# An S5/H3 mix on one core: the first chunk's folds transposed on TensorE, its key spectra ahead of the second phase, loads and columns of the beginning in another order

## The chip, the cores and the metric

The kernel runs on one core of a Trainium2 chip. The metric is the device time of one execution in microseconds (us); of several runs the median counts. Before the change it is 411.53 us, the median of 3 runs from 411.17 to 412.74 us.

## The reference

The input is a sequence `x` of 2048 rows with 1024 columns. Two branches are computed from it and mixed by a gate per row.

```python
g = sigmoid((x * gate_w).sum(-1, keepdims=True))
# A: a diagonal complex state space, 1024 states, one step per row
Lam_bar = exp(dt * Lam);  B_bar = ((Lam_bar - 1) / Lam)[:, None] * Bmat
h[t] = Lam_bar * h[t-1] + B_bar @ x[t]
a = 2 * real(Cmat @ h) + x * Dskip
# B: a short convolution over k, times v, then a long one over 2048 rows
k_shift = sum over t of 4 taps: k shifted by t rows * shift_k[:, t]
kv = k_shift * v
b = x * (irfft(rfft(kv) * rfft(ssm_k)) + kv * ssm_D)
out = g * a + (1 - g) * b
```

All inputs and the output are bfloat16.

## The kernel before, in words

**Branch A** is cut into 8 residues of the row number (`M = 8`, 256 rows each) and 4 groups of states (`NG = 4`, 256 states each, real and imaginary parts apart). `load_xT(r)` brings the rows of residue r turned by a transposing transfer. `step_unit(g, r)` (tiles `bu`) multiplies them with the prepared input matrices `BT`, 32 matmuls of 256 columns, adds the state of residue r-1 by 4 matmuls with `L`, and ScalarE copies the result to `h`. After residue 7 the state `z` goes through `scan(g)`; for all groups but the last it needs a second copy `zs` with its halves exchanged, which two transfers make that ScalarE's queue starts. `carry` (tiles `psT`) brings the scanned state into the other residues; some of these are spilled to memory from ScalarE's queue (`h_scr`) and loaded again later. `Cy` (tiles `psy`) is the output matrix; it fills the last third of the run.

**Branch B** works on 8 chunks of 128 channels. For each chunk `load_k`, `load_v` and `load_kn` bring k, v and the long kernel; `tap_unit` (tiles `taps`) does the short convolution on TensorE, `times_v` multiplies by v on VectorE. The long convolution is done by transforms of length 1024 on blocks. `fold` adds and subtracts the halves of each block on VectorE (two tiles of 128x1024), and each of the two results is turned by a transposing transfer (SBUF to SBUF, 256 KB) into `eok` (kernel) or `eov` (sequence). `spectrum_unit("K" or "V", c, cc, h)` multiplies these with the tables `CF` and `SF`, 4 matmuls of 512 columns, and ScalarE copies the result to `Kr`, `Ks` (or `Kt`) or `Vh`. `products` is the long VectorE chain (`Kp`, `G`, `tmp`, `T`), and `inverse` (tiles `psz`, then `cv`) goes back to rows and spills them to `cv_scr`, again from ScalarE's queue.

**Beginning.** `state_columns` makes the columns of branch A (tiles `cw`, `cols`), `vectors` and `more_vectors` turn small rows into columns on TensorE (tile `psp`): `pcol`, the taps `tcol` and `dcol`, the gate's column `gz`, and `sDc`. `forward_tables` makes `CF` and `SF`. `matrices(g)` makes the tiles `L` of a group on VectorE, `B_unit(q)` multiplies the loaded rows `Bst` with `L` (tiles `psB`, 8 matmuls of 128 columns) and ScalarE copies the result to `BT`.

**The gate.** `gate(r)` multiplies residue r with `gz`; ScalarE copies the row (`grow`) to SBUF, and four small transfers of GpSimd's queue put it into `glog`.

**What sets the order.** Every instruction of an engine is bound to follow the one recorded before it (`put`, line 97), so each engine works off its list in the order written. After the beginning two phases are interwoven: `weave(A[0:NS], first)` mixes the first residues of branch A with the spectra of chunk 0, and the eight periods that follow mix the rest of branch A with `period(c)`. Where a piece stands is a fraction in the table `AT` (line 929): a fraction of the period's matmul weight for branch B (`p0` to `p10` are the steps of `products`, `K00` to `V11` spectra, `fk` the kernel's fold, `lk`, `lv`, `ln` the loads), a residue's number with decimals for the rest. PSUM is one pool of four tiles of two banks, which all of these share. The transfers that SyncE's and ScalarE's queues start are counted on eight semaphores in turn, so that a transfer can be started when the one that had its semaphore before has landed; an engine whose queue holds such a start waits there with all that stands behind it. The pool `s2` has 33 tiles of 2 KB per partition; the gate's row is one of them, and the pool of `cv` has two.

Of the kernel before, what the change touches and what calls it, by code (L numbers as in the profile page):

```python
# [20 lines left out]
def kernel(  # L21
# [169 lines left out]
    small(skr, B_shift_k.rearrange("(j p) k -> j p k", p=128))  # L191
# [49 lines left out]
    def more_vectors():  # L241
        for k in range(KS):
            for h in range(2):
                o = (2 * h + k // 2) * ND
                p0 = 64 * (k % 2)
                mm(psp[p0:p0 + 64, 0, o:o + ND], skr[:, 64 * h:64 * h + 64, k], ident[0:ND, 0:ND], True, True)
        for k in range(KS):
            mm(psp[:, 0, 96 + k:97 + k], skr[:, :, k], ident[0:ND, 0:1], True, True)
        mm(psp[:, 0, 64:64 + 2 * ND], gsr, ident[0:2 * ND, 0:2 * ND], True, True)
        copy(tcol, psp[:, 0, 0:KS * ND].rearrange("p (i j) -> p i j", j=ND))  # L250
        copy(dcol, psp[:, 0, 96:96 + KS])
        copy(gz[:, :, 0], psp[:, 0, 64:64 + ND])
# [61 lines left out]
    def state_columns():  # L314
# [342 lines left out]
    def gate(r):  # L657
# [4 lines left out]
        row = s2([128, K], "grow", F32)  # L662
# [257 lines left out]
    def rows(ts_):  # L920
# [47 lines left out]
        "first": (0.399, 0.45, 0.47, 0.49, 0.51, 0.491, 0.55, 0.57),  # L968
        "gate": (1.261, 3.605, 2.943, 3.887, 4.018, 5.053, 7.446),
        "tabs": ((3.2, 5.821, 6.755, 7.95), (3.928, 5.78, 5.164, 5.561), (1.135, 4.206, 5.313, 6.2), (2.709, 3.396, 5.357, 3.91)),  # L970
        "scan": ((3.375,), (1.2, 1.461, 1.701, 4.5, 3.628, 5.574, 6.459, 6.5, 6.55, 7.5), (1.2, 1.493, 2.127, 4.5, 4.269, 6.764, 6.988, 6.5, 6.55, 7.596), (3.324, 2.57, 2.902, 5.617, 1.123, 5.385, 6.891, 6.921, 3.889, 7.5)),
        "B": ((3.393, 2.536, 7.95, 6.523, 6.218), (3.197, 4.6, 5.6, 7.631, 7.722), (4.107, 4.517, 4.004, 5.925, 7.95)),
        "C": (0.0, 0.394, 0.0, 3.014, 5.724, 0.126, 6.899, 7.218), "tailC": (0.228, 0.188),
# [241 lines left out]
```

## Time and profile before

| what | before |
|---|---|
| median of 3 runs | 411.53 us (411.17 to 412.74) |
| the profiled execution: its own time | 413.82 us |
| its span, first to last instruction | 412.0 us |
| mean granted TensorE clock | 0.984 |
| TensorE busy | 382.3 us (93%), 2598 matmuls |
| VectorE busy | 327.3 us (79%) |
| ScalarE busy | 247.7 us (60%) |
| moved by the transfers | 66.56 MB, 162 GB/s on average |

Rows of a timeline give the start, the duration, the engine (SPq, ACTq: an instruction of that engine's queue that starts a transfer), the operation with its tiles, how many of them are merged (x16), and in brackets how long the engine stood idle before it and what released it. A merged row lasts from its first start to its last end. Rows of windows give, for a stretch, each engine's busy time with its instructions, the granted TensorE clock (PEclk, 1.00 is full), the busy share of the 16 transfer engines and their GB/s.

### The profile page before, as it was taken

The numbers are of one execution on the slowest core, as the hardware profiler recorded it, in microseconds if no ns is written. First come the engines' busy times: TensorE is split into PE (matmuls) and PEld (weight loads), VectorE is DVE, ScalarE is ACT, GpSimd is POOL, SyncE is SP. The second block draws the span as 40 slices with busy tenths as digits, with TensorE's granted clock in tenths as the row PEclk, the third lists the DMA queues.
The fourth block names the chain that finished last, engine by engine and source line by source line (L and its number), as shares of the span: only waits on it lengthen the run. The fifth ranks groups of instructions, "written<-read, shape, count | busy, mean of one in ns | idle before, by whom it ended". The sixth has DMA issues, their size and how long they took to land.

```text
span 412.0 us, 6722 instructions
## 1 busy us (share of the span) xinstructions
PE 382.3 (93%) x2598; PEld 237.8 (58%) x2598; DVE 327.3 (79%) x421; ACT 247.7 (60%) x317; POOL 37.2 (9%) x77
## 2 busy tenths in 40 slices
PE   2979998999998699999998899999999999999994
PEld 1546877576766476787766665354544444444442
DVE  6846869989979699829884886999699899757754
ACT  5637577858793476765653976266833638165671
POOL 2201001224601220100012000100000000000000
PEclk9989999999999699999999999999999999999998
DMA  8999999998199737922999969993664200778862
GB/s 158 203 195 242 200 223 176 196 187 193 29 184 290 117 27 173 210 53 76 201 212 190 147 144 197 247 197 99 144 184 113 86 18 0 212 220 237 221 184 76
DMA packets 140496, 66.56 MB, mean 162 GB/s; under 512 B 121896, under 2 KB 128048, under 8 KB 140464
## 3 DMA queue, kind: packets, MB, share of 16 engines
q1 hardware_dynamic: 131920, 51.66, 60.6%
q0 software_dynamic: 3888, 6.33, 8.9%
q10 hardware_dynamic: 4656, 8.15, 6.9%
q8 instruction: 20, 0.33, 0.3%
q14 instruction: 12, 0.10, 0.1%
HBM read 19.68 MB, written 11.01 MB: 74 GB/s over the span
## 4 chain that ended last, share of the span: by engine, by line
PE 68%; DVE 11%; DMA 10%; ACT 6%; issue 2%; SPq 1%; ACTq 1%; POOL 1%; DVEq 0%; POOLq 0%
PE psy L99 24%; PE bu L99 22%; PE psV L99 5%; PE psz L99 5%; PE psK L99 5%; DMA xT<-in_A_x_dram 4%; PE psT L99 3%; DVE G L99 3%; DMA eov<-vfold 3%; PE taps L99 2%; DVE tmp L99 2%; DMA CT<-CT 2%; DVE T L99 1%; SPq L99 1%; DMA eok<-kfold 1%
## 5 line engine op out<-in xcount | busy, mean ns | idle before, releaser
L99 PE MATMUL bu<-xT,BT 128*128 128x256 bf16 x1024 | 120.2, 277 | 7.1 <-DMA xT<-in_A_x_dram 3.1
L99 PEld LDWEIGHTS <-BT 128*128 128x128 bf16 x1024 | 101.0, 99 | 26.5 <-issue 7.0
L99 PE MATMUL psy<-CT,h 128*128 128x512 bf16 x448 | 98.8, 379 | 0.7 <-DMA CT<-Cim 0.7
L99 PEld LDWEIGHTS <-h 128*128 128x128 bf16 x448 | 43.8, 98 | 53.8 <-DMA CT<-Cim 1.2
L99 ACT ACTIVATE h<-bu 128x1024 bf16<-128x1024 f32 x28 | 28.6, 1022 | 47.9 <-PE bu L99 45.4
L99 ACT ACTIVATE Vh<-psV 128x1024 bf16<-128x1024 f32 x32 | 31.5, 1033 | 5.0 <-PE psV L99 2.5
L99 DVE TENSOR_TENSOR G<-G,tmp 128x3072 bf16<-128x3072 bf16 (+2 forms) x24 | 29.4, 1225 | 0.8
L99 DVE TENSOR_TENSOR T<-T,tmp 128x3072 bf16<-128x3072 bf16 (+2 forms) x24 | 29.4, 1225 | 0.8
L99 ACT ACTIVATE h<-psT 128x1024 bf16<-128x1024 f32 x28 | 27.6, 1027 | 3.6 <-PE psK L99 1.2
L99 DVE TENSOR_TENSOR tmp<-Kp,Vh 128x3072 bf16<-128x3072 bf16 (+2 forms) x24 | 29.3, 1221 | 0.4
L99 POOL DMA_DIRECT2D kk<-kk x21 | 11.1, 532 | 189.7 <-DMA kk<-in_B_k_dram 149.5
L99 ACT ACTIVATE cv<-psz 128x1024 bf16<-128x1024 f32 x16 | 16.5, 1029 | 15.1 <-PE psz L99 7.7
L99 PE MATMUL psT<-h,ident 128*128 128x256 bf16 x112 | 25.4, 272 | 0.0
L99 PEld LDWEIGHTS <-L 128*128 128x128 bf16 x224 | 21.9, 98 | 4.5 <-issue 1.0
L99 PE MATMUL psz<-T,CI 128*128 128x512 bf16 x64 | 24.3, 379 | 0.0
L99 PE MATMUL psz<-T,SI 128*128 128x512 bf16 x64 | 24.3, 379 | 0.0
L99 PEld LDWEIGHTS <-CF 128*128 128x128 bf16 x128 | 12.4, 99 | 18.5 <-issue 6.5
L99 ACT ACTIVATE pairx<-pairx,omg 128x1024 bf16<-128x1024 bf16 (+1 forms) x12 | 11.6, 965 | 18.5 <-DMA pairx<-cv_scr 18.5
L99 DVE TENSOR_TENSOR G<-Kr,Vh 128x4096 bf16<-128x4096 bf16 x8 | 18.3, 2287 | 4.8 <-ACT Vh L99 4.8
L99 PE MATMUL taps<-kk,w 128*64 128x512 bf16 (+1 forms) x128 | 19.8, 402 | 2.0 <-ACT w L99 1.9
L99 PE MATMUL psK<-eok,CF 128*128 128x512 bf16 x64 | 16.9, 394 | 4.8 <-ACT grow L99 4.8
L99 PEld LDWEIGHTS <-SF 128*128 128x128 bf16 x128 | 11.9, 98 | 15.4 <-issue 4.1
(154 smaller groups left out, 574.8 us busy)
## 6 DMA issues: line engine op xcount, KB each, us to landing
kn<-in_B_ssm_k_dram SPq DMA_DIRECT2D x8, 512.0 KB, 4.1
cv_scr<-cv ACTq DMA_DIRECT2D x16, 256.0 KB, 3.2
kk<-kk POOLq DMA_DIRECT2D x14, 255.9 KB, 5.4
h_scr<-h ACTq DMA_DIRECT2D x10, 256.0 KB, 4.5
h<-h_scr SPq DMA_DIRECT2D x10, 256.0 KB, 3.2
CT<-Cim SPq DMA_DIRECT2D x16, 128.0 KB, 3.5
out_dram<-ga SPq DMA_DIRECT2D x16, 128.0 KB, 1.9
Bst<-in_A_B_re_dram SPq DMA_DIRECT2D x14, 128.0 KB, 3.3
```

The lines of the kernel that those rows point to most:

```text
L99: i = f(*a, **kw)
```

## The change

It has five parts.

1. The two folds of chunk 0 (`fold_first`) are no longer turned by transfers. VectorE makes both sums as before; each is multiplied, in 8 pieces of 128 columns, with the unit matrix on TensorE (tiles `psf`, 16 matmuls of 128 columns per fold and 32 in all), and ScalarE copies the four results to `eok` and `eov`.
2. The four key spectra of chunk 0 stand in the beginning, between the fold of the kernel and that of the sequence, and ahead of the second phase, which now interweaves only the four spectra of the sequence.
3. The loads of the beginning are reordered: the kernel `kn` right behind the first `xT`, then the third B rows, v, the fourth B rows, and three `xT` in a row; `B_shift_k` is loaded from SyncE's queue and no longer from ScalarE's. `more_vectors`, `state_columns` and `forward_tables` are cut at other places: `dcol`, `gz` and `sDc` behind VectorE's phase columns, `tcol` at the end of the beginning (its PSUM tile is kept until then), the tables `CF` and `SF` ahead of the tap units' copies. Of `matrices(0)` only the first tile is made ahead of the B units, which are split: two, the fold of the kernel, one, the spectra, the fold of the sequence, one.
4. The gate's row is taken from the two tiles of `cv` and no longer from `s2`.
5. Nearly all places in `AT` are new.

```diff
-    small(skr, B_shift_k.rearrange("(j p) k -> j p k", p=128))
+    move(skr, B_shift_k.rearrange("(j p) k -> j p k", p=128))
...
-        copy(tcol, psp[:, 0, 0:KS * ND].rearrange("p (i j) -> p i j", j=ND))
+        yield
         copy(dcol, psp[:, 0, 96:96 + KS])
         copy(gz[:, :, 0], psp[:, 0, 64:64 + ND])
         copy(sDc, psp[:, 0, 64 + ND:64 + 2 * ND])
+        yield
+        copy(tcol, psp[:, 0, 0:KS * ND].rearrange("p (i j) -> p i j", j=ND))
...
+    def fold_first(hi, lo, name):
+
+        eo = cbuf([128, 2, 4, 2, 128], "eo" + name)
+        fs = []
+        for op in (ALU.add, ALU.subtract):
+            fs.append(s2([128, 4, 256], name + "f"))
+            tt(fs[-1], hi, lo, op)
+        yield
+        for e, f in enumerate(fs):
+            ps = ps2([128, 8, 128], "psf")
+            for k in range(8):
+                mm(ps[:, k], flat(f)[:, 128 * k:128 * k + 128], ident, k % 4 == 0, k % 4 == 3)
+            act(eo[:, e].rearrange("p a m d -> p (a m) d"), ps, func=ACT.Copy)
+        {"k": eoks, "v": evs}[name][0] = eo
...
-        row = s2([128, K], "grow", F32)
+        row = cv_pool.tile([128, K], F32, name="grow", tag="cv")
...
-        "fk": {0: 0.679, 1: 0.504, 7: 0.812, 3: 0.304, 2: 0.146, 5: 0.703, 6: 0.639, 4: 0.494},
+        "fk": {0: 0.648, 1: 0.282, 7: 0.956, 3: 0.304, 2: 0.146, 5: 0.782, 6: 0.351, 4: 0.419},
...
     load_B(0, small)
+    load_B(1, small)
     load_k(0)
     load_xT(0)
-    load_B(1, small)
+    load_kn(0)
     load_B(2)
+    load_v(0)
     load_B(3)
-    load_kn(0)
-    load_v(0)
     load_xT(1)
+    load_xT(2)
...
-    matrices(0)
-    for q in range(4):
-        B_unit(q)
-    fold_k(0)
-    step(ft)
-    load_xT(2)
+    matrices(0, (0,))
+    fk = fold_k0()
+    step(fk)
+    run(ft)
+    B_unit(0)
+    B_unit(1)
+    run(fk)
+    B_unit(2)
+    for cc in range(2):
+        for h in range(2):
+            spectrum_unit("K", 0, cc, h)
+    run(mv)
     times_v(0)
-    fold_v(0)
+    fv = fold_v0()
+    step(fv)
+    matrices(0, (2, 4))
+    run(fv)
+    B_unit(3)
     load_xT(3)
-    run(ft)
```

ScalarE in the beginning, from the copies of the tap units (`ks`) to the first states `h`; `BT` are the input matrices, `eok` and `eov` the turned folds, `hf`, `CF` and `SF` the tables. Before:

```order
L99 ACTIVATE ks<-taps 128x1024 x2
L99 ACTIVATE grow<-p 128x2x128
L99 ACTIVATE BT<-psB 128x1024 x4
L99 ACTIVATE hf<-rq 128x512
L99 ACTIVATE CF<-hf,pih 128x2x256
L99 ACTIVATE SF<-rq 128x2x256
L99 ACTIVATE h<-bu 128x1024 x2
L99 ACTIVATE Kr<-psK 128x2x4x128 x2
L99 ACTIVATE Ks<-psK 128x2x4x128 x2
L99 ACTIVATE Vh<-psV 128x2x4x128 x4
```

and with the change:

```order
L99 ACTIVATE ks<-taps 128x1024 x2
L99 ACTIVATE grow<-p 128x2x128
L99 ACTIVATE BT<-psB 128x1024 x2
L99 ACTIVATE eok<-psf 128x1024 x2
L99 ACTIVATE BT<-psB 128x1024
L99 ACTIVATE Kr<-psK 128x2x4x128 x2
L99 ACTIVATE Ks<-psK 128x2x4x128 x2
L99 ACTIVATE eov<-psf 128x1024 x2
L99 ACTIVATE BT<-psB 128x1024
L99 ACTIVATE Vh<-psV 128x2x4x128 x3
L99 ACTIVATE h<-bu 128x1024 x2
```

The tables went ahead of `ks`, four copies of folds came in, and the fourth `BT`, without which no first state can be formed, now stands behind the four copies of key spectra and behind all four folds.

SyncE's queue in the beginning, from the fourth B rows to the second load of `kn`, as one piece of the difference (`xT` are the turned rows of a residue, `vT` is v turned):

```order
-L99 DMA kn<-in_B_ssm_k_dram 128x2048
-L99 DMA_TRANSPOSE vT<-in_B_v_dram 128x2048
-L99 DMA_TRANSPOSE xT<-in_A_x_dram 128x8x256
-L99 DMA_TRANSPOSE eok<-kf 128x8x128 x2
-L99 DMA_TRANSPOSE xT<-in_A_x_dram 128x8x256
-L99 DMA_TRANSPOSE eov<-vfold 128x8x128 x2
-L99 DMA_TRANSPOSE xT<-in_A_x_dram 128x8x256
+L99 DMA_TRANSPOSE xT<-in_A_x_dram 128x8x256 x3
```

The four turned folds are gone from the queue, and `kn` and `vT` stand further ahead.

SyncE's queue later, in the second group's last residues, the transfers of chunks 3 and 4 that end with the fold `eov` of chunk 3. Before:

```order
L99 DMA Bst<-in_A_B_re_dram 64x1024
L99 DMA Bst<-in_A_B_im_dram 64x1024
L99 DMA_TRANSPOSE eok<-kfold 128x8x128 x2
L99 DMA kn<-in_B_ssm_k_dram 128x2048
L99 DMA Bst<-in_A_B_re_dram 64x1024
L99 DMA Bst<-in_A_B_im_dram 64x1024
L99 DMA_TRANSPOSE kk<-in_B_k_dram 128x2048
L99 DMA_TRANSPOSE vT<-in_B_v_dram 128x2048
L99 DMA_TRANSPOSE eov<-vfold 128x8x128 x2
```

and with the change:

```order
L99 DMA_TRANSPOSE eok<-kfold 128x8x128 x2
L99 DMA Bst<-in_A_B_re_dram 64x1024
L99 DMA Bst<-in_A_B_im_dram 64x1024
L99 DMA_TRANSPOSE kk<-in_B_k_dram 128x2048
L99 DMA Bst<-in_A_B_re_dram 64x1024
L99 DMA Bst<-in_A_B_im_dram 64x1024
L99 DMA kn<-in_B_ssm_k_dram 128x2048
L99 DMA_TRANSPOSE vT<-in_B_v_dram 128x2048
L99 DMA_TRANSPOSE eov<-vfold 128x8x128 x2
```

The pair `eok` went ahead of both pairs of B rows, and `kk` ahead of `kn`; `vT` and `eov` are still the last two.

More of the change, by code (lines that the diff above doesn't have):

```diff
@@ L348, in state_columns @@
         tt(tl, tl, tr, ALU.subtract)
+        tt(II, ident[:, 0:64], ident[:, 64:128], ALU.add)
+        ts(jrow, jrow_i, 0.5, None, ALU.mult)
         yield
@@ L418, in fold_k, with fold @@
         hi, lo = kb[:, :, 1], kb[:, :, 0, ::-1]
-        eoks[c] = fold(hi, lo, "k", c == 0)
-    def fold(hi, lo, name, first=False):
+        eoks[c] = fold(hi, lo, "k")
+    def fold(hi, lo, name):
         eo = cbuf([128, 2, 4, 2, 128], "eo" + name)
         for e, op in enumerate((ALU.add, ALU.subtract)):
-            f = s2([128, 4, 256], "kf") if first else fold_pool.tile([128, 4, 256], BF16, name=name + "fold", tag="f")
+            f = fold_pool.tile([128, 4, 256], BF16, name=name + "fold", tag="f")
             tt(f, hi, lo, op)
@@ L459, in fold_v, with fold_k0, fold_v0 @@
         evs[c] = fold(kb[:, :, 1], kb[:, :, 0, ::-1], "v")
+    def fold_first(hi, lo, name):
[11 more added lines that the diff above has]
+        {"k": eoks, "v": evs}[name][0] = eo
+    def fold_k0():
+        kn = lds.pop(("kn", 0))
+        tt(kn[:, 0:1], kn[:, 0:1], sDc[:, 0:1], ALU.add)
+        kb = kn.rearrange("p (a h t) -> p a h t", a=4, h=2)
+        return fold_first(kb[:, :, 1], kb[:, :, 0, ::-1], "k")
+    def fold_v0():
+        kb = kss[0].rearrange("p (a h t) -> p a h t", a=4, h=2)
+        return fold_first(kb[:, :, 1], kb[:, :, 0, ::-1], "v")
     def spectrum_unit(which, c, cc, h):
@@ L929 @@
     AT = {
[38 rows of a table removed]
[L968 to L973, printed above, removed]
-        "tailS": (0.0, 0.446, 0.005, 1.22, 0.0, 1.104, 0.163, 0.262, 1.952, 2.0),
[29 rows of a table removed]
[38 rows of a table added]
+        "first": (0.038, 0.0, 0.584, 0.168), "gate": (0.184, 3.444, 1.97, 3.456, 5.383, 5.053, 7.214),
+        "tabs": ((3.2, 4.258, 6.522, 7.95), (3.928, 5.78, 5.091, 5.672), (0.0, 3.825, 5.313, 6.2), (2.634, 4.327, 5.39, 3.91)),
+        "scan": ((1.535,), (1.2, 1.461, 1.701, 4.397, 3.628, 5.574, 6.459, 6.5, 6.55, 7.5), (1.027, 1.493, 2.127, 4.5, 4.269, 6.764, 6.988, 6.994, 6.536, 7.596), (3.324, 2.861, 3.571, 5.617, 1.123, 5.048, 6.88, 6.621, 3.828, 7.5)),
+        "B": ((3.393, 3.131, 7.684, 5.345, 6.218), (3.197, 4.6, 5.6, 7.707, 7.95), (4.107, 4.517, 4.166, 5.925, 7.95)),
+        "C": (0.173, 0.394, 0.392, 3.375, 0.163, 0.483, 5.365, 6.473), "tailC": (0.0, 0.187),
+        "tailS": (0.047, 0.579, 0.048, 1.471, 0.0, 0.93, 0.144, 0.556, 1.816, 2.0),
[30 rows of a table added]
     }
@@ L1071 @@
     load_B(0, small)
+    load_B(1, small)
     load_k(0)
     load_xT(0)
-    load_B(1, small)
+    load_kn(0)
     load_B(2)
+    load_v(0)
     load_B(3)
-    load_kn(0)
-    load_v(0)
     load_xT(1)
-    sc, ft, it = state_columns(), forward_tables(), inverse_tables()
+    load_xT(2)
+    sc, ft, it, mv = state_columns(), forward_tables(), inverse_tables(), more_vectors()
     step(ft)
     vectors()
+    step(mv)
     step(sc)
-    more_vectors()
+    step(mv)
     tap_weights(0)
     step(sc)
-    step(sc)
+    step(ft)
     tap_unit(0, 0)
@@ L1116 @@
     first = [(AT["first"][i], w, f) for i, (w, f) in enumerate((
-        (WK, later(spectrum_unit, "K", 0, 0, 0)),
-        (WK, later(spectrum_unit, "K", 0, 0, 1)),
-        (WK, later(spectrum_unit, "K", 0, 1, 0)),
-        (WK, later(spectrum_unit, "K", 0, 1, 1)),
         (WK, later(spectrum_unit, "V", 0, 0, 0)),
```

3 lines of the change are left out of this document (removed), and 133 rows, old and new, of the table AT.

## The prediction

> **What bounds the kernel now.** First the page's busy times:
>
> ```profile
> span 412.0 us, 6722 instructions
> PE 382.3 (93%) x2598; PEld 237.8 (58%) x2598; DVE 327.3 (79%) x421; ACT 247.7 (60%) x317; POOL 37.2 (9%) x77
> ```
>
> TensorE is busy 382.3 of 412.0 us, so at most 29.7 us of idle time can be won, and every added matmul costs unless it fills a hole. Second, TensorE's waits, largest first (total, how often, longest):
>
> ```profile
> PE p L99 <- DVE rows L99: 5.3, 1, 5.3
> PE psK L99 <- ACT grow L99: 4.8, 1, 4.8
> PE bu L99 <- DMA xT<-in_A_x_dram: 3.1, 1, 3.1
> ```
>
> They are few, and each is one event. The first lies ahead of everything the change moves; the second and third are what it can win. Third, the timeline of the beginning (SPq: SyncE's queue):
>
> ```profile
> 8.36 1.26 ACT L99 ACTIVATE w<-ident,dcol 128x128 bf16<-128x128 bf16 x4
> 8.80 5.66 PE L99 MATMUL taps<-kk,w 128*128 128x512 bf16 x16 [1.85 <-ACT w L99]
> 14.73 1.96 PE L99 MATMUL psB<-L,Bst 128*128 128x128 bf16 x32
> 15.70 3.78 ACT L99 ACTIVATE BT<-psB 128x1024 bf16<-128x1024 f32 x4
> 16.78 3.80 PE L99 MATMUL bu<-xT,BT 128*128 128x256 bf16 x32
> 19.29 3.10 SPq L99 DMA_TRANSPOSE eok<-kf  x2
> 19.38 1.23 DVE L99 TENSOR_TENSOR ks<-ks,vT 128x2048 bf16<-128x2048 bf16 x1 [0.94 <-DMA vT<-in_B_v_dram]
> 20.64 1.29 DVE L99 TENSOR_TENSOR vfold<-ks 128x1024 bf16<-128x1024 bf16 x2
> 23.68 5.08 PE L99 MATMUL bu<-xT,BT 128*128 128x256 bf16 x32 [3.11 <-DMA xT<-in_A_x_dram]
> 24.72 2.75 SPq L99 DMA_TRANSPOSE eov<-vfold  x2
> 29.03 1.89 PE L99 MATMUL psK<-eok,CF 128*128 128x512 bf16 x8
> 33.77 3.82 ACT L99 ACTIVATE Vh<-psV 128x1024 bf16<-128x1024 f32 x4
> 35.94 3.66 PE L99 MATMUL bu<-xT,BT 128*128 128x256 bf16 x32
> ```
>
> Residue 1's `bu` waits 3.11 us for its `xT`, then its 32 matmuls last 5.08 us against 3.66 in residue 2. The windows say why (PE, PEld, DVE, ACT, POOL, then PEclk, DMA share, GB/s):
>
> ```profile
> 23.70:27.00 3.30, 3.30 (x18) 2.40 (x19) 1.63 (x2) 0.00 (x0) 0.00 (x0) 0.56 1.08 238
> 27.00:29.00 2.00, 2.00 (x21) 1.79 (x19) 0.00 (x0) 0.00 (x0) 0.00 (x0) 1.00 0.90 167
> ```
>
> After that pause the granted clock was 0.56, and within 3.3 us it was full again. Fourth, the largest movable wait, at 132 us (ACTq: ScalarE's queue):
>
> ```profile
> 113.17 4.18 SPq L99 DMA_TRANSPOSE eok<-kfold  x2
> 117.44 0.53 SPq L99 DMA_DIRECT2D kn<-in_B_ssm_k_dram  x1
> 119.33 2.76 SPq L99 DMA_TRANSPOSE kk<-in_B_k_dram  x1
> 120.92 1.29 DVE L99 TENSOR_TENSOR vfold<-ks 128x1024 bf16<-128x1024 bf16 x2
> 122.19 3.24 SPq L99 DMA_TRANSPOSE vT<-in_B_v_dram  x1
> 125.60 7.27 SPq L99 DMA_TRANSPOSE eov<-vfold  x2
> 131.19 5.37 ACTq L99 DMA_DIRECT2D zs<-z  x2
> 136.60 0.40 ACT L99 ACTIVATE grow<-p 128x256 f32<-128x256 f32 x1 [5.45 <-DMA eov<-vfold]
> 137.05 1.86 PE L99 MATMUL psK<-eok,CF 128*128 128x512 bf16 x4 [4.75 <-ACT grow L99]
> 138.71 5.59 PE L99 MATMUL bu<-xT,BT 128*128 128x256 bf16 x32
> ```
>
> SyncE starts five transposing transfers one behind the other. The chain of waits gives the last one 10.47 us, so it lands at 136.07:
>
> ```profile
> 125.60 10.47 DMA eov<-vfold
> ```
>
> ScalarE wants to start `zs`, whose semaphore is the one of `eov`; it stands 5.45 us, with `grow` behind it, and TensorE waits 4.75 us for the PSUM tile of `grow`. Then it is cold: four `psK` take 1.86 us (half of the eight in 1.89 would be 0.95, so 0.9 more), the `bu` 5.59 instead of 3.66 (1.9 more). The stall costs 4.75 + 0.9 + 1.9 = **7.5 us**.
>
> **The change part by part.** *Beginning.* Removed are four transposing transfers (1 MB; 3.10 + 2.75 us of SyncE's queue) and, with `xT` of residue 1 now behind no fold, the 3.11 us wait and its cold matmuls. But the first state is formed later: the last `BT` now stands behind four fold copies and four key spectra. From 15.70 ScalarE has 12 copies in a row (three `BT`, four folds, four key spectra, the last `BT`); by 3.78 / 4 = 0.95 us each they last 11.4 us, to 27.1. TensorE's work beside it (32 `psB` 1.96, 32 fold matmuls of the same shape 1.96, key spectra 2 x 1.89, three of the four pairs of V spectra or so) is some 8.6 us and fits: the 1.96 us that are added cost nothing while ScalarE sets the pace, and all of 1.96 if it does not. The three V spectra that stand ahead of the first states are through about 27.8. Then come two residues of `bu` (2 x 3.66) and the fourth V spectrum (half of 1.89), 8.3 in all; merged rows end with a latency that the next group overlaps, so the four small matmuls of residue 1's state are not added. Residue 2 starts at about 36.1 where it started at 35.94. **+0.2 us**. Below: if ScalarE's copies wait less than counted, -0.8; above: the beginning keeps its length and only the added 1.96 and the wait's remains come on top, +2.5. I take the middle sum, since each of its terms has a row. Covers: `xT` 1 is needed at about 31 instead of 23.7; `vT` was there at 19.4, and `ks` and the fold (1.23 and half of 1.29) must be done before ScalarE reaches `eov` at 24, so it may be 2.7 us late before anything waits; `kn`, now behind the first `xT`, is used no earlier than before. `w` waits for `dcol`, which now sits behind VectorE's phase columns; `w` starts at 8.36 today, and a delay there would move the whole front one to one.
>
> *The glut.* SyncE's order is now `eok` first, then B rows, `kk`, `kn`, `vT`, `eov`. Where the pair `eok` was started at 113.17, its place is some 11 us earlier, into a stretch with free transfer engines:
>
> ```profile
> 100.00:120.00 20.00, 20.00 (x174) 13.89 (x174) 17.00 (x19) 16.92 (x22) 9.32 (x18) 1.00 0.51 82
> 120.00:140.00 20.00, 15.25 (x120) 10.55 (x119) 16.18 (x17) 9.36 (x11) 3.72 (x7) 0.90 1.15 234
> ```
>
> The DMA share is 0.51 at 82 GB/s before 120 and 1.15 at 234 GB/s behind it. The pair is 0.5 MB: at 234 GB/s 2.2 us less stand in front of `eov`. SyncE's 4.18 us for it are gone from 113 on, and `kk` no longer waits for `kn`, but `eov` cannot start before `vfold` ends at 120.92 + 1.29 = 122.2, 3.4 us earlier than 125.60. So `eov` lands 2.2 to 5.2 us earlier (3 of start, 2.2 of bytes), and of ScalarE's 5.45 us 0.2 to 3.2 stay, middle 1.7. TensorE's wait was 0.7 shorter than ScalarE's, so 1.0 stays, too short to cool it: a wait of 1.68 us, below, was followed by `bu` at full pace. I take 7.5 - 1.1 = **-6.4 us**. Bounds: 0 if `eov` lands no earlier, -7.5 if all goes; -4.9 with 3.2 of hold left.
>
> *The gate's row* now shares two tiles with `cv`. A later `cv` must wait until the four small transfers have read the row, which stand in POOL's queue behind two `H`:
>
> ```profile
> 81.64 2.15 POOL L99 DMA_DIRECT2D H<-a  x2 [2.08 <-DVE H L99]
> 85.89 1.02 ACT L99 ACTIVATE cv<-psz 128x1024 bf16<-128x1024 f32 x1
> ```
>
> 2.15 for `H`, as much again for the row's four, and a landing of about 3.3 us end at `H` + 7.6; `cv` was copied at `H` + 4.25. ScalarE may be held 1 to 3 us, which two blocks of `bu` on TensorE (2 x 3.66) hide: 0. If the cover is gone it is up to 3.4, of the kind in the next bound.
>
> *New places.* Nearly every piece moves. The stall at 222 us has the same build after the change (`cv`'s spill still queues on the semaphore of an `eov`):
>
> ```profile
> 221.78 1.02 ACT L99 ACTIVATE cv<-psz 128x1024 bf16<-128x1024 f32 x1 [6.93 <-DMA eov<-vfold]
> 222.85 3.65 PE L99 MATMUL bu<-xT,BT 128*128 128x256 bf16 x32 [1.68 <-ACT cv L99]
> 228.10 3.65 PE L99 MATMUL bu<-xT,BT 128*128 128x256 bf16 x32 [1.59 <-ACT Kr L99]
> ```
>
> No row shows what moved places do. Below: both waits go, -1.7 - 1.6 = -3.3. Above: one more stall as long as today's largest, +4.75. I take the middle, **+0.8**, since neither end is nearer.
>
> Sum: +0.2 - 6.4 + 0.8 = **-5.4**. The profiled execution's own time is 413.82, 2.3 above the median of the runs; the sum goes onto its span, 412.0 to 406.6 (its own time to 408.4), and the same difference onto the median: 411.5 - 5.4 = **406.1 us**.
>
> **The rivals.** *The glut stays* (1): the bytes, not their order, set when `eov` lands. For it: 234 GB/s behind 120 us, whatever the queue does. Against: the stretch before has half its share free. Then +0.2 + 0.8 = 412.5.
>
> *Given back later* (2): TensorE comes 5.4 us earlier to 217 us, the transfers do not, and the hold behind `eov` grows. For it, the window there:
>
> ```profile
> 216.00:220.00 4.00, 4.00 (x37) 3.50 (x36) 3.90 (x8) 0.00 (x0) 0.52 (x1) 1.00 1.35 214
> 224.00:228.00 4.00, 2.51 (x23) 2.09 (x22) 0.82 (x2) 3.67 (x10) 0.00 (x0) 1.00 1.30 122
> ```
>
> The DMA share is 1.30 to 1.35. Against: the loads there are started by a queue that moves with the work. If all transfers stay, all 5.4 are lost, 411.5; if half move along, 408.8; I put it at 410.4.
>
> *Slower: a half clock in the front* (3). Between 15.7 and 36 us TensorE works in groups of 0.5 to 1 us between ScalarE's copies, and nothing long lets it warm. If the clock falls to half there and stays, 8.6 us of work become 17.2 in a stretch of 12, +5.2, and two residues of `bu` another 7.3: +12.5 - 5.4 = 418.6; warm again after 3.3 us as in the windows above, it is about +5. It decides if the clock is still half at 23 us. Against: 224 to 228 was 2.51 of 4.00 busy, with a clock of 1.00.
>
> The Trainium skill, "TensorE: Matmul & The Clock Gate", section "A second HAM failure mode: psum-queue depth-cycling", names this: short pauses between PSUM groups can make the clock oscillate. The trace so far speaks against it, by the row just named.
>
> **How the numbers follow.** About 2 us (0.5%) is what a measurement here tells from no change: 409.5 to 413.6. The forecast gets 0.56, all faster. (1) gets 0.12, nearly all within; (2) 0.14, of it 0.10 within and 0.04 faster; (3) 0.10, slower; 0.08 is left for what none of them names, half faster, half not. Faster 0.63, within 0.22, slower 0.15. The forecast's own range: 402.0 (both later waits go too) to 409.5 (3.2 of the hold stays, and a new stall of 2). Reaching to (1) gives **402.0 to 412.6**; (3) and part of the rest stay outside.
>
> **What would show it.** Front: ScalarE without a hole from 15.7 to about 27, `bu` of residue 2 near 36, a clock of 1.00 between; half clock at 23 us or later speaks for (3). Glut: no wait of `psK` for `grow`, ScalarE not held at `zs` for over 3.2 us, `eov` landing within 4 to 7 us of its start; if it still takes 10, (1). The waits of `bu` for `cv` and `Kr` at 217 to 223 us stay at 1 to 2 us; at 5, (2). No hold of `cv` behind `glog` over 3 us. The forecast is wrong if TensorE's idle time, 29.7 us now, is not below 27, or if a wait over 3 us stands where none stood.

## The result and the profile after

| | before | changed |
|---|---|---|
| median of 4 runs | 411.50 us (411.17 to 412.74) | 407.32 us (405.71 to 408.37) |
| the profiled execution: its own time, span | 413.82, 412.0 us | 408.37, 406.6 us |
| mean granted TensorE clock | 0.984 | 0.998 |
| TensorE busy, idle | 382.3, 29.7 us | 379.7, 26.9 us |

The changed kernel is faster by 1.1%: ratio 0.989, 95% interval 0.9851 to 0.9929. The medians differ by 4.2 us and the two profiled spans by 5.4 us. Two more timings on other chips, told below, gave 0.9946 (0.9876 to 1.0015, which includes no change) and, with the gate's row in `s2` again, 0.9909 (0.9866 to 0.9952). The gain is thus some 2 to 4.5 us, in each of the three less than the 5.4 us that were forecast. In the experiments below executions of one and the same kernel lie up to 16 us apart (the kernel before: 406.3 to 422.0), so the medians there are over all executions, while the ratios, by which faster or slower is told, leave out those over 1.5% above the fastest of their kernel.

The page of the changed kernel, to be set beside the two lines of the kernel before:

```profile
span 406.6 us, 6769 instructions
PE 379.7 (93%) x2630; PEld 238.2 (59%) x2630; DVE 326.7 (80%) x421; ACT 251.2 (62%) x321; POOL 37.2 (9%) x77
```

32 matmuls were added (rows `psf` of 1.36 and 1.06 us), and TensorE is busy 2.6 us less: the matmuls that ran at a lower clock before are shorter now. Its waits (in all, times, longest):

```profile
PE bu L99 <- ACT Kr L99: 2.9, 1, 2.9
PE psy L99 <- DMA CT<-Cim: 2.8, 2, 1.8
...
PE taps L99 <- DMA kk<-kk: 1.6, 1, 1.6
PE psK L99 <- ACT BT L99: 1.6, 1, 1.6
PE psV L99 <- ACT eov L99: 1.2, 1, 1.2
PE psK L99 <- ACT eok L99: 0.8, 1, 0.8
PE psK L99 <- ACT grow L99: 0.6, 1, 0.6
```

The 4.8 us for `grow` are 0.6, the 3.1 us for `xT` are gone, `CT` has 2.8 us where it had 0.7, and 1.6 us for `kk` are new. The beginning, from the timeline:

```profile
15.32 1.94 ACT L99 ACTIVATE BT<-psB 128x1024 bf16<-128x1024 f32 x2
17.12 1.98 ACT L99 ACTIVATE eok<-psf 128x1024 bf16<-128x1024 f32 x2
18.23 1.89 PE L99 MATMUL psK<-eok,CF 128*128 128x512 bf16 x8 [0.78 <-ACT eok L99]
...
23.45 2.06 ACT L99 ACTIVATE eov<-psf 128x1024 bf16<-128x1024 f32 x2
...
25.26 1.17 ACT L99 ACTIVATE BT<-psB 128x1024 bf16<-128x1024 f32 x1
26.16 3.02 ACT L99 ACTIVATE Vh<-psV 128x1024 bf16<-128x1024 f32 x3
...
27.23 7.15 PE L99 MATMUL bu<-xT,BT 128*128 128x256 bf16 x64
...
35.52 3.66 PE L99 MATMUL bu<-xT,BT 128*128 128x256 bf16 x32
```

and the same stretch by windows (PE, PEld, DVE, ACT, POOL, then clock, DMA share, GB/s):

```profile
15.30:27.20 11.90, 9.67 (x84) 5.89 (x83) 9.96 (x16) 11.90 (x15) 2.29 (x4) 1.00 1.13 199
```

ScalarE is busy in 11.90 of 11.90 us: it sets the pace here, TensorE has 9.67 us of work beside it, and the clock is 1.00. At 100 to 134 us:

```profile
98.56 5.08 SPq L99 DMA_TRANSPOSE eok<-kfold  x2
111.30 1.90 SPq L99 DMA_TRANSPOSE kk<-in_B_k_dram  x1
...
114.75 0.59 SPq L99 DMA_DIRECT2D kn<-in_B_ssm_k_dram  x1
117.53 1.04 POOL L99 DMA_DIRECT2D kk<-kk  x2 [1.82 <-DMA kk<-in_B_k_dram]
119.30 2.76 SPq L99 DMA_TRANSPOSE vT<-in_B_v_dram  x1
122.22 4.94 SPq L99 DMA_TRANSPOSE eov<-vfold  x2
122.55 0.52 POOL L99 DMA_DIRECT2D kk<-kk  x1 [3.98 <-DMA kk<-kk]
...
131.62 1.13 ACTq L99 DMA_DIRECT2D zs<-z  x2
133.30 1.02 PE L99 MATMUL psK<-eok,CF 128*128 128x512 bf16 x4 [0.57 <-ACT grow L99]
134.20 3.88 PE L99 MATMUL bu<-xT,BT 128*128 128x256 bf16 x32
```

`eok` starts 14.6 us earlier than before, `kk` 8.0, `eov` 3.4. ScalarE starts both `zs` in 1.13 us instead of 5.37, `psK` waits 0.57 us and is not cold (1.02 against 1.86), nor is `bu` behind it (3.88 against 5.59). The three differences are 4.18 + 0.84 + 1.71 = 6.7 us. The rows of GpSimd's queue, `kk<-kk`, are the three transfers with which `load_k` shifts k inside SBUF for the short convolution; they play a part below. The stall at 217 us stays:

```profile
215.35 1.02 ACT L99 ACTIVATE cv<-psz 128x1024 bf16<-128x1024 f32 x1 [6.48 <-DMA eov<-vfold]
221.56 3.65 PE L99 MATMUL bu<-xT,BT 128*128 128x256 bf16 x32 [2.88 <-ACT Kr L99]
```

### The profile page after: what moved, and what is told of

It is laid out like the page before. It is cut to its first block, busy times and chain, and to the rows that moved or that the text cites. A ratio compares the mean times of both kernels' runs of the same rounds, so it can differ in the third digit from the quotient of the medians.

```text
span 406.6 us, 6769 instructions
## 1 busy us (share of the span) xinstructions
PE 379.7 (93%) x2630; PEld 238.2 (59%) x2630; DVE 326.7 (80%) x421; ACT 251.2 (62%) x321; POOL 37.2 (9%) x77
## 4 chain that ended last, share of the span: by engine, by line
PE 55%; DVE 8%; ACT 4%; DMA 4%; issue 4%; SPq 1%; ACTq 1%; DVEq 0%; POOLq 0%
PE psy L99 24%; PE bu L99 15%; PE psz L99 4%; PE psV L99 4%; PE psK L99 3%; DVE G L99 3%; PE psT L99 3%; DMA CT<-CT 2%; PE taps L99 2%; ACT h L99 1%; DMA kk<-kk 1%; DVE tmp L99 1%; DVE a L99 1%; SPq L99 1%; DVE T L99 1%
## 5 line engine op out<-in xcount | busy, mean ns | idle before, releaser
L99 PE MATMUL bu<-xT,BT 128*128 128x256 bf16 x1024 | 116.9, 273 | 3.2 <-ACT Kr L99 2.9
L99 PEld LDWEIGHTS <-BT 128*128 128x128 bf16 x1024 | 99.6, 98 | 20.8 <-issue 5.3
L99 POOL DMA_DIRECT2D glog<-grow x32 | 18.1, 651 | 36.8 <-ACT grow L99 35.4
L99 ACT ACTIVATE gd<-drow,glog 128x512 bf16<-128x512 bf16 (+1 forms) x25 | 20.7, 827 | 0.0
```

What stands on the lines that cost most here:

```text
L99: i = f(*a, **kw)
```

## The experiments

Theory at the start: the stall at 132 us was what the change won, through the order of SyncE's queue there (`eok` early, `kk` ahead of `kn`); the beginning itself is worth little. First rival: the shifted beginning dissolved the stall. Below, "before" is the median of the kernel before, timed beside the experiment on the same chip.

**The beginning alone.** The changed kernel with the old table `AT` (its `first` apart) and the old place of the gate's row.

```diff
-        row = cv_pool.tile([128, K], F32, name="grow", tag="cv")
+        row = s2([128, K], "grow", F32)
...
-        "p0": {0: 0.023, 5: 0.146, 6: 0.15, 7: 0.097, 4: 0.0, 3: 0.051, 2: 0.068, 1: 0.224},
+        "p0": {0: 0.127, 5: 0.195, 6: 0.154, 7: 0.017, 4: 0.0, 3: 0.0, 2: 0.135, 1: 0.224},
...
```

> The kernel with the new beginning alone: turned folds on TensorE, key spectra ahead, loads and columns reordered; the table of places and the gate's row as before. Theory (the beginning itself is worth little, the stall at 132 us is what was won): residue 2's bu starts at 35.5 us as in the changed kernel (35.94 before), the wait of psK for grow near 135 us stays at 4 to 5 us, and the time is 411.1 us, 0 to 1 below before. Rival (shifting the beginning is what dissolved the later stall): the wait is under 1.5 us and the time is 404 to 407 us.

Measured: 411.45 us, before 413.93; ratio 1.0022 (0.9972 to 1.0072). The wait of `psK` for `grow` is 4.24 us, residue 2 starts at 35.96, residue 4 at 44.27 (45.13 before). The rival falls: with the new beginning the stall stands where it stood. What the beginning is worth by itself cannot be told from nothing by the interval.

**SyncE's order alone, in the kernel before.** One number, then two. TensorE's and ScalarE's lists stay the same word for word.

```diff
-        "fk": {0: 0.679, 1: 0.504, 7: 0.812, 3: 0.304, 2: 0.146, 5: 0.703, 6: 0.639, 4: 0.494},
+        "fk": {0: 0.679, 1: 0.282, 7: 0.812, 3: 0.304, 2: 0.146, 5: 0.703, 6: 0.639, 4: 0.494},
```

> The kernel before with one number changed: the fold of chunk 3's kernel at 0.282 of its period instead of 0.504, so that its pair eok is started some 10 us earlier; TensorE and ScalarE have the same lists. Theory (2.2 us of bytes and SyncE's 4.2 us leave the front of eov, but kn still stands ahead of kk): eov lands 2 to 5 us earlier than 136.07, psK's wait for grow falls from 4.75 to 0 to 2.5 us, time 405.5 to 409 us. Rival 1 (the bytes behind 120 us set the landing whatever the order): wait 4 us or more, 411 to 412 us.

Besides it, in the second:

```diff
-        "ln": {0: 0.996, 6: 0.979, 7: 0.252, 3: 0.63, 5: 0.943, 2: 0.522, 4: 0.559, 1: 0.64},
+        "ln": {0: 0.996, 6: 0.979, 7: 0.252, 3: 0.63, 5: 0.943, 2: 0.522, 4: 0.559, 1: 0.835},
```

> As the run before, and the load of kn at 0.835 instead of 0.64, behind that of kk: SyncE's list at this place is then the one of the changed kernel, word for word, in the kernel before. Theory: the stall is gone, wait under 1 us, bu behind it at 3.7 instead of 5.59 us, all of 7.5 us but what later waits take back: 404 to 406.5 us. Rival 2 (given back at 214 to 228 us, where the transfers do not move along): waits there grow from 3.3 to over 6 us and the time is 409.5 to 411.5 us.

Measured: the first 409.28 us, before 413.93 (ratio 0.9981, 0.9936 to 1.0026), with a wait of 0.99 us for `grow`. The short wait wins little: TensorE comes to this place at 135.11 us, 2.8 us later than in the kernel before, and `psK` starts at 136.10, only 1.0 us earlier. The second took 413.20 us (ratio 1.0067, 1.0014 to 1.0119) and is slightly slower. Unlike what was expected of it, it does not have SyncE's order of the changed kernel: `kk` stands behind both pairs of B rows, where the changed kernel has it between them, and `kn` starts 1.7 us ahead of `vT`, where the changed kernel has 4.6. Its timeline, with the last B rows:

```profile
114.17 0.59 SPq L99 DMA_DIRECT2D Bst<-in_A_B_im_dram  x1
114.94 3.68 SPq L99 DMA_TRANSPOSE kk<-in_B_k_dram  x1
118.67 0.58 SPq L99 DMA_DIRECT2D kn<-in_B_ssm_k_dram  x1
120.37 2.75 SPq L99 DMA_TRANSPOSE vT<-in_B_v_dram  x1
121.33 1.04 POOL L99 DMA_DIRECT2D kk<-kk  x2 [6.50 <-PE psV L99]
123.29 10.09 SPq L99 DMA_TRANSPOSE eov<-vfold  x2
...
140.04 0.40 ACT L99 ACTIVATE grow<-p 128x256 f32<-128x256 f32 x1 [7.30 <-DMA eov<-vfold]
140.49 1.86 PE L99 MATMUL psK<-eok,CF 128*128 128x512 bf16 x4 [6.60 <-ACT grow L99]
```

`eov` starts 2.3 us earlier than in the kernel before, and the wait is longer, 6.60 us. `vT` takes 12.2 us to land, where it took 4.8 in the changed kernel and 7.1 before. What runs beside it are the shifts `kk<-kk` and the load of `kn`. So these two numbers alone are not enough. The full order of the changed kernel is put into the kernel before further below, with an earlier second tap unit.

**The same two numbers undone in the changed kernel.**

```diff
-        "fk": {0: 0.648, 1: 0.282, 7: 0.956, 3: 0.304, 2: 0.146, 5: 0.782, 6: 0.351, 4: 0.419},
+        "fk": {0: 0.648, 1: 0.504, 7: 0.956, 3: 0.304, 2: 0.146, 5: 0.782, 6: 0.351, 4: 0.419},
...
-        "ln": {0: 0.896, 6: 0.979, 7: 0.0, 3: 0.63, 5: 0.909, 2: 0.522, 4: 0.607, 1: 0.835},
+        "ln": {0: 0.896, 6: 0.979, 7: 0.0, 3: 0.63, 5: 0.909, 2: 0.522, 4: 0.607, 1: 0.64},
```

> The changed kernel with those two numbers as before (fold of chunk 3's kernel at 0.504, load of kn at 0.64). Theory: psK's wait for grow near 133 us comes back with 3 to 5 us and a cold clock behind it, time 411 to 414 us. Rival (other new places keep the stall away by themselves): 406.5 to 408.5 us.

Measured: 419.75 us, before 413.93, ratio 1.022 (1.015 to 1.0289): slower than the kernel before.

```profile
121.33 6.18 SPq L99 DMA_TRANSPOSE vT<-in_B_v_dram  x1
122.34 1.04 POOL L99 DMA_DIRECT2D kk<-kk  x2 [8.07 <-PE psz L99]
127.69 12.34 SPq L99 DMA_TRANSPOSE eov<-vfold  x2
...
143.15 1.86 PE L99 MATMUL psK<-eok,CF 128*128 128x512 bf16 x4 [11.88 <-ACT grow L99]
```

So the changed kernel needs these places, and the price without them is above the 3 to 5 us of wait that were expected. `vT` took 19.5 us to land, again beside `kk<-kk`, with `kn` and a pair of B rows started within 2 us ahead of it. The windows compare what is moved. From 120 to 142 us this kernel's transfer engines are busy at a share of 1.16 and move 176 GB/s; the changed kernel from 117 to 133 us moves 239 GB/s at 1.06. But the kernel before, with its stall, moves 244 GB/s at 1.16 from 119 to 136 us, so there an excess of bytes is not excluded. The three, in this order:

```profile
120.00:142.00 22.00, 11.27 (x100) 8.20 (x98) 12.57 (x13) 5.83 (x6) 1.56 (x3) 0.85 1.16 176
```

```profile
117.00:133.00 16.00, 15.73 (x133) 11.42 (x131) 15.24 (x15) 10.44 (x12) 1.56 (x3) 1.00 1.06 239
```

```profile
119.00:136.00 17.00, 13.30 (x116) 9.78 (x114) 14.90 (x15) 7.85 (x8) 1.56 (x3) 1.00 1.16 244
```

**A second theory: collision** (theory C in the expectations). The shifts `kk<-kk` and the transposing `vT` and `eov` would slow each other when they run together. In the kernel before they run side by side:

```profile
125.58 1.04 POOL L99 DMA_DIRECT2D kk<-kk  x2 [12.35 <-DMA kk<-in_B_k_dram]
```

that is in the same moment as `eov` (125.60). In the changed kernel the first two start at 117.53, 1.8 us ahead of `vT`; the third starts at 122.55, beside `eov` there too. The rival is that the bytes alone count: the three shifts are 768 KB, by the 244 GB/s above some 3 us (an estimate). Three experiments go with it: the kernel with the long stall and the kernel before, each without the three shifts of chunk 4, and the kernel before with both numbers and an earlier second tap unit, which frees the buffer of `kk`.

```diff
-        if c == 0:
+        if c in (0, 4):
             return
         hop(kk[0:64, 1, PAD:], kk[64:128, 0, PAD:])
```

> The changed kernel with chunk 3's fold and the load of kn late, which took 419.75 us with a wait of 11.88 us of psK for grow; here it also leaves out the three transfers kk<-kk that shift k of chunk 4 (768 KB; chunk 4's short convolution then works on wrong rows, so part of the computation is missing). Theory C: the wait falls under 2.5 us and the time to 407 to 410.5 us, though kk, vT, kn and both pairs of folds are started as late as there. Rival 1 (bytes alone: 0.77 MB less at some 200 GB/s are 3.8 us): wait 7 to 9 us, 414.5 to 417 us.

> The kernel before without the three transfers kk<-kk of chunk 4 (chunk 4's short convolution then works on wrong rows, so part of the computation is missing), all else as it is. Theory C: eov lands within 7 us of its start instead of 10.5, psK's wait for grow falls from 4.75 to under 1.5 us, the spread becomes narrow and the median is 404 to 408 us. Rival 1 (bytes: 3.8 us at most): wait 1 to 4 us, 409 to 411 us, spread as before.

Measured: the kernel with the long stall 414.10 us (its six executions 411.4 to 416.3; with the shifts, on another chip, 417.7 to 420.2), ratio to before 1.0129 (1.0037 to 1.0222); the kernel before 410.47 us against 415.01, ratio 0.9971 (0.9907 to 1.0035). Their timelines, the first without the long stall:

```profile
120.64 4.12 SPq L99 DMA_TRANSPOSE vT<-in_B_v_dram  x1
124.93 5.51 SPq L99 DMA_TRANSPOSE eov<-vfold  x2
...
136.37 1.83 PE L99 MATMUL psK<-eok,CF 128*128 128x512 bf16 x4 [4.75 <-ACT grow L99]
```

and the kernel before without shifts:

```profile
128.02 4.36 SPq L99 DMA_TRANSPOSE eov<-vfold  x2
...
136.07 1.02 PE L99 MATMUL psK<-eok,CF 128*128 128x512 bf16 x4 [1.18 <-ACT grow L99]
```

In the first TensorE comes to this place at the same time with and without shifts (131.62 and 131.27 us), so the two waits can be compared: they are 4.75 and 11.88 us, and the shifts cost 7.1 us there, more than the 3 us of their bytes. But 4.75 us stay with no shift in the way, `vT` still takes 12.6 us, and the transfer engines move 187 GB/s, hardly more than the 176 with shifts:

```profile
120.00:142.00 22.00, 17.25 (x136) 12.33 (x135) 19.24 (x19) 10.33 (x12) 2.11 (x4) 0.92 0.96 187
```

The wait lies between theory C (under 2.5) and the rival (7 to 9); the time misses theory C by 3.6 us and the rival by 0.4. In the kernel before, the waits of 4.75 and 1.18 us can't be subtracted: without shifts TensorE comes 2.6 us later (134.89 against 132.30), and `psK` starts at 136.07, 1.0 us earlier than with them. `eov` landed at most 7.6 us after its start, against 10.5. The wait fits theory C and the rival, and the time (409 to 411) and the spread, as wide as before (406.2 to 418.0), are the rival's. So collision is not shown for the kernel before: bytes would do as much.

The kernel before with both numbers (`fk` and `ln`), and besides:

```diff
-        "t1": {0: 0.034, 1: 0.661, 7: 0.928, 6: 0.67, 3: 0.648, 5: 0.62, 4: 0.65, 2: 0.645},
+        "t1": {0: 0.034, 1: 0.61, 7: 0.928, 6: 0.67, 3: 0.648, 5: 0.62, 4: 0.65, 2: 0.645},
```

> The kernel before with fold and kn placed as in the run with both numbers changed (fold 0.282, kn 0.835), and besides the second tap unit of chunk 3 at 0.61 instead of 0.661, as in the changed kernel, which frees the buffer of kk earlier. Theory C: kk starts 2 to 3 us earlier than there (114.9), its shifts are started by 119 us and over when eov runs, psK's wait is under 1.5 us, and the median is 405.5 to 409 us with a narrow spread. Rival 1: no change against that run (413 us).

Measured: 411.19 us, before 415.01, ratio 0.9979 (0.9912 to 1.0045).

```profile
114.63 1.26 SPq L99 DMA_TRANSPOSE kk<-in_B_k_dram  x1
...
119.72 1.04 POOL L99 DMA_DIRECT2D kk<-kk  x2 [2.63 <-DMA kk<-in_B_k_dram]
...
135.45 1.13 ACTq L99 DMA_DIRECT2D zs<-z  x2
...
137.07 1.02 PE L99 MATMUL psK<-eok,CF 128*128 128x512 bf16 x4 [0.51 <-ACT grow L99]
```

Here SyncE's order at this place is the one of the changed kernel: `kk` stands between the two pairs of B rows and `kn` behind them. ScalarE is not held, and starts both `zs` in 1.13 us; the shifts start 4.6 us ahead of `vT`, and the wait for `grow` is 0.51 us. The glut is gone as the prediction said. But TensorE comes to this place at 136.56 us, 4.3 us later than before, 1.9 of it from a longer wait for `psB` near 45 us, ahead of everything that this edit moves; and `psK` starts at 137.07, where it started in the kernel before (137.05). The median lies 2 us above the expected range, and the ratio does not tell a gain from no change.

The changed kernel unaltered, timed beside these three:

> The changed kernel unaltered, beside the kernel before in the same call, since the four experiments before this one were timed in a call in which the kernel before spread from 406 to 422 us. New theory C (collision: the transfers kk<-kk, with which GpSimd's queue shifts k of chunk 4, slow the transposing vT and eov when they run beside them; the changed kernel starts them at 117.5 us and has them off the road before vT, the kernel before starts them at 125.6 us beside eov): narrow spread, 405.5 to 409 us, all of its gain against the median of before. Rival 1 (order and bytes alone): the changed kernel spreads as widely as the one before, 404 to 418 us.

Measured: 408.56 us, before 415.01; ratio 0.9946 (0.9876 to 1.0015), median lower by 6.5 us. It spreads from 405.15 to 413.71, the kernel before from 407.8 to 419.9: not narrow, as theory C had it. By standard deviation the two spread alike, 3.1 and 3.0 us, the changed kernel in 12 executions and the other in 29. The ratio comes to 2.2 us, and its interval includes no change. The profile has the wait of 0.57 us again, and neither the 1.6 us for `kk` nor the 2.8 us for `CT` of the first profile: its span is 403.7 us.

**One number back in the changed kernel**: the second tap unit of chunk 3.

```diff
-        "t1": {0: 0.0, 1: 0.61, 7: 0.468, 6: 0.602, 3: 0.685, 5: 0.62, 4: 0.66, 2: 0.621},
+        "t1": {0: 0.0, 1: 0.661, 7: 0.468, 6: 0.602, 3: 0.685, 5: 0.62, 4: 0.66, 2: 0.621},
```

> The changed kernel with one number as before: the second tap unit of chunk 3 at 0.661 instead of 0.61, so that kk starts later and behind one more pair of B rows; the fold of chunk 3's kernel stays early, kn stays behind kk. Theory C (the early kk is what keeps the shifts off vT and eov): kk starts 3 to 5 us later than 110 to 111, its shifts run beside vT, psK's wait for grow is 2 to 6 us and the time 410.5 to 414 us. Rival 1 (the early eok and kn behind kk are enough): wait under 1 us, 407 to 409.5 us.

Measured: 411.52 us, before 413.36; ratio 0.997 (0.993 to 1.001). `kk` starts at 116.31, the shifts at 123.30, 1.8 us behind `vT`; the first `eov` takes 10.2 us. TensorE waits 0.73 us for `grow` and 1.18 us for the next `BT` copy, less than theory C said, since it comes there 2.4 us later than in the changed kernel. `vT` lands in 6.3 us all the same. The wait is the rival's (under 1), the median lies in the range of theory C, 2.8 us above the changed kernel with the row in `s2` (408.73, next), which was timed beside it; by the ratios it is 2.5 us, and the intervals overlap. So this run does not decide.

**The gate's row in `s2` again.**

```diff
-        row = cv_pool.tile([128, K], F32, name="grow", tag="cv")
+        row = s2([128, K], "grow", F32)
```

> The changed kernel with the gate's row in s2 again, all else as changed. Theory (the row's place is worth nothing; what it may hold on ScalarE is hidden by bu): within 1 us of the changed kernel's 408.56, so 407 to 410 us, no wait of TensorE over 0.5 us that was not there. Rival (the two tiles of cv make a wait that costs TensorE): 1.5 to 4 us faster, 404.5 to 407 us.

Measured: 408.73 us, before 413.36; ratio 0.9909 (0.9866 to 0.9952). The changed kernel's 408.56 comes from another timing on another chip, so the two can't be set against each other to a microsecond; no cost or gain of the row's place shows.

**The turn by TensorE undone**: chunk 0's folds go through transfers, `eok` ahead of `xT` 1, `eov` behind it.

```diff
             tt(fs[-1], hi, lo, op)
+            load_t(eo[:, len(fs) - 1].rearrange("p a m d -> p (a m) d"), flat(fs[-1]))
         yield
-        for e, f in enumerate(fs):
-            ps = ps2([128, 8, 128], "psf")
-            for k in range(8):
-                mm(ps[:, k], flat(f)[:, 128 * k:128 * k + 128], ident, k % 4 == 0, k % 4 == 3)
-            act(eo[:, e].rearrange("p a m d -> p (a m) d"), ps, func=ACT.Copy)
...
-    load_xT(1)
-    load_xT(2)
...
     step(fk)
+    load_xT(1)
...
     step(fv)
+    load_xT(2)
```

> The changed kernel with chunk 0's folds turned by transfers again, eok ahead of xT of residue 1 on SyncE's queue and eov behind it. Theory (the turn on TensorE buys latency in the beginning, not work): eok lands at 20 us or later instead of being copied by 19.1, eov at 27 or later instead of 25.5, residue 2 starts at 37 to 40 us (35.5 with TensorE), time 1.5 to 5 us above the changed kernel: 410 to 413.5 us. Rival (ScalarE's chain of copies, now four shorter and 3.8 us less, sets the beginning): residue 2 starts at 34 us or earlier and the time is 405 to 408 us.

Measured: 414.85 us, before 413.36; ratio 0.9977 (0.9919 to 1.0036), 6.1 us above the changed kernel with the row in `s2` (408.73; 0.9866 to 0.9952), timed beside it. By the ratios it is 2.8 us, and their intervals overlap slightly.

```profile
21.29 3.59 PE L99 MATMUL psK<-eok,CF 128*128 128x512 bf16 x8 [4.99 <-DMA eok<-kf]
...
38.69 3.66 PE L99 MATMUL bu<-xT,BT 128*128 128x256 bf16 x32
```

The spectra wait 4.99 us for `eok` and then run cold (3.59 against 1.89), residue 2 starts 3.2 us later than in the changed kernel, and residue 4 5.4 us later (49.25 against 43.83), after 2.1 us of waiting ahead of a `psB`. The loss by the ratios lies within the 1.5 to 5 us expected, by the medians above. The rival (ScalarE's chain, four copies shorter, would start residue 2 at 34) falls.

**A version aimed at the stall at 217 us**: the tap units of chunk 5 earlier.

```diff
-        "t0": {0: 0.788, 1: 0.491, 3: 0.609, 2: 0.5, 6: 0.565, 7: 1.0, 5: 0.543, 4: 0.399},
-        "t1": {0: 0.0, 1: 0.61, 7: 0.468, 6: 0.602, 3: 0.685, 5: 0.62, 4: 0.66, 2: 0.621},
+        "t0": {0: 0.788, 1: 0.491, 3: 0.55, 2: 0.5, 6: 0.565, 7: 1.0, 5: 0.543, 4: 0.399},
+        "t1": {0: 0.0, 1: 0.61, 7: 0.468, 6: 0.602, 3: 0.6, 5: 0.62, 4: 0.66, 2: 0.621},
```

> The changed kernel with the tap units of chunk 5 at 0.55 and 0.60 of their period instead of 0.609 and 0.685, which frees the buffer of kk earlier; kk and kn then stand ahead of two transfers of CT. The stall that both kernels have at 217 to 222 us (cv's spill behind eov, TensorE 2.9 to 3.0 us for Kr) is the one aimed at. Theory C (the shifts of kk beside vT and eov make that landing late): kk starts 2 to 4 us earlier than 195, eov lands 2 us earlier, TensorE's wait falls under 1.5 us, time 405.5 to 407.5 us, faster than both kernels. Rival (eov waits there for what is computed or for the transfers of CT): wait 2.5 to 4 us as before, 408 to 410 us.

Measured: 410.42 us, before 413.36; ratio 0.9961 (0.9918 to 1.0004). It does not beat the changed kernel: `kk` starts at 195.1 as before, `eov` at 214.7 instead of 208 to 210, and TensorE waits 4.36 us for `Kr`. The edit did not move what it was to move, so it says nothing on collision there.

## Why the prediction was right, point by point

**The time.** Predicted 406.1 us (402.0 to 412.6), measured 407.3. On the span the sum was 406.6 us, and 406.6 was measured. That it fits to the tenth is luck: a second profile of the changed kernel has 403.7, and the three terms miss by -0.6, -0.3 and +0.9, which cancel. The profiled execution of the kernel before was 2.3 us above its median, the one of the changed kernel 1.0, which is the difference between 406.1 and 407.3. The signs of being wrong stayed away by little: TensorE's idle time is 26.9 us ("not below 27"), and the longest wait behind the beginning 2.9 ("over 3").

**The beginning, +0.2.** Measured -0.4 (35.52 against 35.94). The steps hold: ScalarE without a hole until 26.4 (predicted 27.1), V spectra through at 27.4 (27.8), clock 1.00. But this is one pair of profiles. The five with the old beginning have residue 2 at 33.9 to 35.9 us, 34.9 on average, and the eight with the new one at 35.5 to 36.7, 36.0 on average: the wait of 3.11 us for `xT` that the sum took away was the longest of the five (1.8 to 3.1). So the change costs 1.1 us at residue 2, within the bounds. The account ended there, and something is won behind it: ahead of residue 4 the old beginning waits 0.7 to 2.9 us for a `psB` and starts it at 44.6 to 45.6 us; the new one, whose B rows are loaded earlier, starts it without a wait at 43.4 to 44.5, 1.2 us earlier. The two nearly cancel, which fits the run of the beginning alone (ratio 1.0022). The half-clock rival is refuted: TensorE paused 0.2 to 1.2 us between groups and stayed at 1.00. By the depth-cycling that the Trainium skill, "TensorE: Matmul & The Clock Gate", section "A second HAM failure mode: psum-queue depth-cycling", describes, the clock could have oscillated there. This trace does not agree: 1.00 throughout.

**The glut, -6.4.** Measured -6.7 in the same three terms. The size was right, the mechanism half. The step that failed is "`eov` lands 2.2 to 5.2 us earlier (3 of start, 2.2 of bytes)": the `eov` on which ScalarE's queue waits landed at 129.08 instead of 136.07, 7.0 us earlier, 3.4 of start and 3.6 of duration (6.9 instead of 10.5 us). Whether the reason given, SyncE's order and the bytes ahead, did this stays open. Put alone into the kernel before, in full with the earlier `kk`, the order freed ScalarE as predicted, but gave no gain that the ratio shows. And the earlier `kk` also moves the shifts of GpSimd's queue away from `eov`: the prediction looked at SyncE's and ScalarE's queues and left these out. That the shifts matter is shown for the kernel with the long stall (11.88 to 4.75 us of wait, with TensorE there at the same time). For the kernel before and the changed one, collision, bytes and the order in SyncE's queue are not separated, nor is which of early `eok`, early `kk` and `kn` behind it is enough.

A wait is the difference of two times, when TensorE comes and when ScalarE is through; what is won is in when the waiting `psK` starts:

| profile | `eov` starts | TensorE comes | wait | `psK` starts |
|---|---|---|---|---|
| before | 125.60 | 132.30 | 4.75 | 137.05 |
| changed | 122.22 | 132.73 | 0.57 | 133.30 |
| changed, second profile | 121.21 | 131.12 | 0.57 | 131.69 |
| changed, row in `s2` | 121.83 | 131.84 | 0.52 | 132.36 |
| changed, tap unit late | 124.38 | 135.14 | 0.73 | 135.87 |
| changed, fold and `kn` undone | 127.69 | 131.27 | 11.88 | 143.15 |
| the same without shifts | 124.93 | 131.62 | 4.75 | 136.37 |
| before, new beginning | 124.72 | 131.44 | 4.24 | 135.68 |
| before, fold early | 125.56 | 135.11 | 0.99 | 136.10 |
| before, fold and `kn` | 123.29 | 133.89 | 6.60 | 140.49 |
| before, fold, `kn`, tap unit | 127.23 | 136.56 | 0.51 | 137.07 |
| before without shifts | 128.02 | 134.89 | 1.18 | 136.07 |

In this table `psK` starts by 133.30 us only in the changed kernel with its places kept; no edit of the kernel before starts it more than 1.4 us earlier than 137.05.

**New places, +0.8.** What is left of the span's -5.4 is +1.7: 1.6 us for `kk` and 2.1 more for `CT` are new, 0.8 of the waits at 222 to 236 us and 1.5 us of waits of `psa` and `psH` for VectorE are gone, and the rest is small. Inside the bounds of -3.3 and +4.75. It is partly chance: the second profile of the same kernel has neither of the two new waits.

**The rivals.** The glut did not stay. *Given back at 217 us* did not happen: 2.9 us are waited there in one piece where it was 1.7 + 1.6. **The gate's row** was rightly put at 0.

**What was wrong in the account of parts.** The removal of the four transfers was costed through the beginning's length alone. With the new order around it, going back to transfers costs 3.2 us at residue 2 and 2.2 more at residue 4, and 2.8 us by the ratios (6.1 by the medians, intervals overlapping), although the beginning as a whole moved residue 2 by 1.1 us at most: with the spectra ahead of the first states, the latency of the turn stands on the path, which the prediction had as nothing but a length of copies. Two figures of the prediction are misread without harm to its conclusions. Its rows show six transposing transfers of SyncE one behind the other (`eok` twice, `kk`, `vT`, `eov` twice), not five. And the work that it names for TensorE beside ScalarE's copies adds up to 10.5 us, not 8.6; 9.67 were measured, and it fits into the 11.90.

## What to carry to other kernels

When a transfer lands late, list all queues that have transfers in flight at that time, GpSimd's too, before its place in its own queue is taken as the cause: here leaving out shifts of another queue took 7.1 us from a wait of 11.88. Compare when the waiting instruction starts, and not only how long it waits: with the order of the changed kernel in the kernel before, the wait fell from 4.75 to 0.51 us and the instruction started at the same time. Two profiles of kernels that are still alike up to some place already differ there (0.7 to 2.9 us of wait for the same `psB` near 45 us in the five with the old beginning), so a change of one place needs many runs beside the old kernel, and a single profile tells only what waited for what. A transfer that is "hidden" still sets the latency of a chain: turning 256 KB on TensorE, which was busy 9.67 of 11.90 us there, put residue 2 3.2 us ahead of the transfers, although it lengthened the list of the engine that set the pace.

## What the hardware showed that was not expected

The same load can land very late. Of the thirteen profiles that show when `vT` (512 KB) of chunk 4 landed, it took 4.8 to 7.4 us in the nine in which `kn` was started at least 4 us ahead of it, the kernel before without shifts among them (7.1 us with and without them). In the other four, with `kn` 1.7 to 1.9 us ahead, it took 12.2 and 19.5 us with the shifts about 1 us behind it, 12.6 with no shifts, and 6.3 with the shifts 1.8 us behind. Neither the shifts nor `kn` alone explains that, and no run separates them. The shifts themselves took 10 and 16 us in the first two instead of 4.

The length of a pause alone does not decide whether TensorE's clock falls. Pauses ahead of a `bu` of 2.00, 2.34 and 3.11 us were followed by a clock of 0.50, 0.51 and 0.56 and `bu` of 5.30, 5.33 and 5.08 us (the kernel before without shifts, with the fold early, and as it is). A pause of 2.88 us in the changed kernel left the clock at 1.00 and the `bu` at 3.65 us.

```profile
21.95 5.30 PE L99 MATMUL bu<-xT,BT 128*128 128x256 bf16 x32 [2.00 <-DMA xT<-in_A_x_dram]
```
